# Start and end of a fused attention and feed-forward kernel: another order of loads and values in the first batch, and the last output tile in two column halves

## The chip, the cores and the metric

The kernel runs on one core of a Trainium2 chip. The metric is the device time of one execution in microseconds (us), taken over several runs of which the median is given. A profile of one further execution shows what each engine did: PE is TensorE's matmuls, PEld its weight loads, DVE is VectorE, ACT is ScalarE, POOL is GpSimd, SP is SyncE, which only issues DMAs here.

## The reference

Attention with two kinds of heads, then a feed-forward network without biases. Sizes: 8 batches, 8 heads, 576 positions, head size 64; 4608 tokens, model width 512, inner width 1024. All inputs and the output are float32.

```python
scores = scale * np.matmul(q, k.transpose(0, 1, 3, 2))
rel = pos[:, None] - pos[None, :]
mask_plain = (rel >= 0) & (rel < 32)                       # heads 0 to 3
mask_dil = (rel >= 0) & (rel < 128) & (rel % 4 == 0)       # heads 4 to 7
attn = softmax of the masked scores                        # rows divided by their sum
x = np.matmul(attn, v)          # then to [4608 tokens, 512 channels]
a = x @ w1;  b = x @ w2
out = ((a * b) @ w3) @ w_out
```

## The kernel before

**Attention in steps.** A batch is four steps: `d0`, `d1` (dilated heads, first and second half of the positions) and `p0`, `p1` (plain heads, likewise). The order of positions is permuted so that a dilated head, too, sees a narrow band; each half is then three blocks of 96 queries by 128 keys. A step is: scores on TensorE into PSUM (`score_matmuls`, L275), the exponential on ScalarE into `et`, the values on TensorE (`value_matmul`, L317) with a column of ones beside V that yields the row sum, the division on VectorE (`normalize`: a reciprocal, L324, and a product, L325, into `xo`), and six transposes on TensorE with a copy into the channel-major array `XT` (`to_channels`, L366 and L380). `transpose_qk` brings q and k into head-size-major form on VectorE, four small instructions each, or a single long one (L240) for k of the plain heads.

**Feed-forward.** Tokens are taken 512 at a time, nine tiles. `ffn1` makes a block of 128 features of `a` and `b`, each from four products of 128x512 (L509), multiplied into `gts`; `ffn2` makes 128 tokens of the output from eight products (L560) with `wf_sb`, which is w3 times w_out, computed on the chip once (`fuse_t`, `fuse_m`). ScalarE copies each output tile y to `osb` (L568), and SyncE stores it (L549), in two DMAs where the tile crosses one of the permuted quarters, else in one.

**Order.** The instruction order is written by hand; each engine works through its own list in program order. For batches 1 to 7 the attention work is handed out piece by piece between the products of the feed-forward part (`point`). Batch 0 has nothing to hide behind. It is written out in `first_batch`: there scores and values go in pairs of heads (`scores_of_pair`, `values_of_pair`), and the mask comes in through a product of the identity with a tile of large negative numbers (L291). When XT of the dilated channels is there, four PSUM banks are opened and `begin` computes the half of the first four products that needs only those channels; `ffn1` finishes them later. `begin` of the first feature block stands ahead of `p0.to_channels`, that of the second between it and `p1.to_channels`. Before all that, `warm_up` runs 16 products on constant data while the first loads are under way.

**Queues and buffers.** All loads are issued by GpSimd, in the order in which the main program calls `load_qk`, `load_vd` (V of the dilated heads, four DMAs of pieces of partitions), `load_vp` (V of the plain heads), `load_w12`, and so on; they convert float32 to bfloat16 on the way. Eight semaphores serve these DMAs in turn, so that an issue waits until the DMA eight places ahead has landed. PSUM: one bank `ps_x` for transposes, three banks in rotation handed out by `bank()`, and four that are first the two score buffers `ps_s` (two banks each), then `ps_b` of `begin`, then `ps_a` of the later attention. A bank from `bank()` is free again when the last reader of its former content is done. `et` has three buffers.

Of the kernel before, what the change touches and what calls it, by code (L numbers as in the profile page):

```python
# [10 lines left out]
P = 128  # L11
BF16 = mybir.dt.bfloat16
F32 = mybir.dt.float32
U32 = mybir.dt.uint32
AL = mybir.AluOpType
# [5 lines left out]
D = 64  # L21
# [6 lines left out]
TB = 512  # L28
# [8 lines left out]
def kernel(  # L37
# [11 lines left out]
    nc = tc.nc  # L49
# [6 lines left out]
    KFF = d_ff // P  # L56
    NT = n_tok // TB
# [6 lines left out]
    wk_pool = ctx.enter_context(tc.tile_pool(name="wk", bufs=2))  # L64
# [18 lines left out]
    wf_sb = const.tile([P, KFF, d_model], BF16, name="wf_sb")  # L83
# [16 lines left out]
    ps_x = psum.tile([P, 2 * TB], BF16, name="ps_x")  # L100
    pool = four_banks()
# [3 lines left out]
    def bank():  # L105
        return banks.tile([P, TB], F32, tag="f", name="f")


    qn, kn = {}, {}

    def load_qk(b, us=slice(0, 2)):
        for nm, dst, src in (("qn", qn, q), ("kn", kn, k)):
            if b not in dst:
                dst[b] = qk_pool.tile([P, 2, ROWS * D], BF16, tag=nm, name=nm)
            x = src[b].rearrange("(u h) (j a) d -> (h j) u (a d)", u=2, a=ROWS)
            nc.gpsimd.dma_start(out=dst[b][:, us], in_=x[:, us])  # L116

    def load_vp(b):
        vp = vps[b % NV]
        base = v[b, 0]  # L120

        def rows(p0, n, j0, nj):
            return bass.AP(
                tensor=base.tensor,
                offset=base.offset + (96 * j0 - 32 + p0) * D,
                ap=[[D, n], [96 * D, nj], [1, D]],
            )

        if b < NV:
            nc.gpsimd.dma_start(out=vp[32:P, 0:1, 0:D], in_=rows(32, 96, 0, 1))  # L130
            nc.gpsimd.dma_start(out=vp[:, 1:24, 0:D], in_=rows(0, P, 1, 23))
        else:
            nc.gpsimd.dma_start(out=vp[:, :, 0:D], in_=rows(0, P, 0, 24))

    def load_vd(b):


        x = v[b, 4]
        for m, p0, n, i0, second in ((0, 32, 96, 0, 0), (1, 0, 80, 64, 0), (1, 80, 48, 0, 1), (2, 0, P, 16, 1)):
            nc.gpsimd.dma_start(  # L140
                out=vds[b % 2][p0 : p0 + n, 4 * m : 4 * m + 4, 16 : 16 + 2 * D],
                in_=bass.AP(
                    tensor=x.tensor,
                    offset=x.offset + (4 * i0 + 2 * second) * D,
                    ap=[[4 * D, n], [S * D, 4], [1, 2 * D]],
                ),
            )
# [26 lines left out]

    def warm_up(n):

        ps = bank()
        for _ in range(n):
            nc.tensor.matmul(
                out=ps, lhsT=warm[:, 0:P], rhs=warm, start=True, stop=True  # L180
            )
# [43 lines left out]
    def const_masks():  # L225
        for mask, neg in ((mask_pl, neg_pl), (mask_di, neg_di)):
            nc.vector.tensor_scalar(
                out=mask, in0=neg, scalar1=-1.0, scalar2=None, op0=AL.is_ge
            )


    def transpose_qk(b, u, which):


        src, dst = ((qn, qts), (kn, kts))[which]
        pad = PADK * which
        t = src[b][:, u, :].bitcast(U32).rearrange("p (a i) -> p a i", a=ROWS)
        o = dst[u][b % 2].rearrange("p s c -> p (s c)").bitcast(U32)[:, pad : pad + S]
        if u == 0 and which == 1:
            nc.vector.transpose(out=o.rearrange("p (j a) -> p a j", a=ROWS), in_=t)  # L240
            return
        for a0 in range(4):

            n = 5 - a0 // 2
            at = RES * SLOTS.index(a0)
            step = RES * SLOTS.index((a0 + 2) % 4) + (a0 + 18) // 4 - at
            nc.vector.transpose(  # L247
                out=bass.AP(
                    tensor=o.tensor,
                    offset=o.offset + at,  # L250
                    ap=[o.ap[0], [1, n], [9, 16], [step, 2]],
                ),
                in_=t[:, a0 : a0 + 4 * n - 3 : 4, :],
            )

    class Step:
# [62 lines left out]
            )  # L319

        def normalize(self, ov, xo, n, k):
            rcp = wk_pool.tile([P, n, k], F32, tag=f"rcp{n}", name="rcp")
            ones, x0 = (0, 1) if self.u and self.hf == 0 else (D, 0)
            nc.vector.reciprocal(out=rcp[0:96], in_=ov[0:96, :, :, ones])  # L324
            nc.vector.tensor_tensor(  # L325
                out=xo[0:96].rearrange("p (n k) d -> p n k d", n=n),
                in0=ov[0:96, :, :, x0 : x0 + D],
                in1=rcp[0:96].unsqueeze(3).to_broadcast([96, n, k, D]),
                op=AL.mult,
            )  # L330

        def new_xo(self):
            self.xo = wk_pool.tile([P, 2, 6, D], BF16, tag="xo", bufs=3, name="xo")

        def values_of_pair(self, hp):
            if hp == 0:
                self.new_xo()
            ov = bank()[:, 0 : 6 * (D + 1)].unsqueeze(1)
            ov = ov.rearrange("p n (j e) -> p n j e", e=D + 1)
            for m in range(3):  # L340
                for hl in range(2):
                    self.value_matmul(2 * hp + hl, m, ov[:, 0, 2 * m + hl, :])
            self.normalize(ov, self.xo[:, hp], 1, 6)

        def values(self):


            self.new_xo()
            ov = late["a"][:, :, HALF : HALF + 3 * (D + 1)]
            ov = ov.rearrange("p n (j e) -> p n j e", e=D + 1)  # L350
            for hp in range(2):
                for m in range(3):
                    for hl in range(2):
                        j = 6 * hp + 2 * m + hl
                        self.value_matmul(2 * hp + hl, m, ov[:, j // 3, j % 3, :])
            self.normalize(ov, self.xo.rearrange("p h j d -> p (h j) d"), 4, 3)

        def to_channels(self, ps=ps_x, copy=None):
            xv = ps[:, 0 : 2 * HALF].rearrange("p (h s t) -> p h s t", h=2, s=4)
# [47 lines left out]
    def first_batch():  # L407

        d0, d1, p0, p1 = steps[0:4]
        transpose_qk(0, 1, 0)  # L410
        transpose_qk(0, 1, 1)
        d0.scores_of_pair(0)
        d0.scores_of_pair(1)
        transpose_qk(0, 0, 0)
        transpose_qk(0, 0, 1)
        d1.scores_of_pair(0)
        d1.scores_of_pair(1)
        p0.scores_of_pair(0)
        p0.scores_of_pair(1)
        d0.values_of_pair(0)  # L420
        d0.values_of_pair(1)
        p1.scores_of_pair(0)
        d1.values_of_pair(0)
        p1.scores_of_pair(1)
        d1.values_of_pair(1)
        d0.to_channels()
        p0.values_of_pair(0)
        p0.values_of_pair(1)
        d1.to_channels()
        p1.values_of_pair(0)  # L430
        p1.values_of_pair(1)
        pool = four_banks()
        for f in range(2):
            for i in range(2):
                begin(f, i, pool.tile([P, TB], F32, name=f"ps_b{f}{i}"))
            if f == 0:
                p0.to_channels()
        p1.to_channels(bank().bitcast(BF16), nc.vector.tensor_copy)
        const_masks()
        prefetch(2)  # L440

# [63 lines left out]
    gts = {}  # L505
# [13 lines left out]
    def begin(f, i, ps):  # L519

        begun[f, i] = ps
        ffn1_half(0, f, (w1_sb, w2_sb)[i], (2, 3), begun[f, i])
# [16 lines left out]
                nc.scalar.copy(out=a_sb, in_=ps)  # L539
        nc.vector.tensor_tensor(out=gts[t][:, f], in0=pss[1], in1=a_sb, op=AL.mult)  # L540

    def store(o_sb, r0):
        n = 0
        while n < P:
            b, p = divmod(r0 + n, S)
            slot, i = divmod(p, RES)
            m = min(P - n, RES - i)
            row = b * S + 4 * i + SLOTS[slot]
            nc.sync.dma_start(  # L549
                out=out[row : row + 4 * (m - 1) + 1 : 4, :], in_=o_sb[n : n + m, :]  # L550
            )
            n += m

    def ffn2(t, tb, point):
        point()
        y = bank()
        for f in range(KFF):
            if f == KFF // 2:
                point()
            nc.tensor.matmul(  # L560
                out=y,
                lhsT=gts[t][:, f, tb * P : (tb + 1) * P],
                rhs=wf_sb[:, f, :],
                start=(f == 0),
                stop=(f == KFF - 1),
            )
        o_sb = wk_pool.tile([P, d_model], F32, tag="osb", bufs=6, name="osb")
        nc.scalar.copy(out=o_sb, in_=y)  # L568
        store(o_sb, t * TB + tb * P)

    w3T = {}

# [30 lines left out]
    warm_up(16)  # L603
    load_qk(0, 1)
    const_pool()
    load_qk(0, 0)
    load_vd(0)
    load_vp(0)
    load_w12(0, 256)
    load_w12(256, 512)  # L610
# [24 lines left out]
    def point():  # L635
        state[0] += 1
        want = int(np.ceil(np.interp(state[0], xs, ys)))
        while state[1] < want and (state[1] >= n0 or state[0] >= when[state[1]]):
            for f in phases[state[1]]:
                f()  # L640
            state[1] += 1
# [11 lines left out]
    for tb in range(4):  # L653
        ffn2(0, tb, point)
# [36 lines left out]
```

The softmax here doesn't subtract the row's maximum and nothing guards it: scores larger than these inputs give would overflow.

## Time and profile before

| | us |
|---|---|
| median of 5 runs | 264.15 |
| lowest, highest | 262.93, 266.75 |
| the profiled execution: its own time | 262.93 |
| its span, first to last instruction | 261.2 |
| TensorE busy in the span | 248.5 (95%) |
| start of the dense stream of products | 20.71 |
| end of the last product | 257.04 |

The profiled execution was one of the quicker ones: its own time is 1.2 us under the median, and 1.7 us of it lie outside of the span that the profile shows. All moments below are counted from the span's start. In a row of the timeline the first number is the start, the second the duration, and the bracket tells how long the engine had been idle and what ended that. Ends of matmuls are modelled, so that TensorE's busy time is not time at its peak.

### The profile page before, as it was taken

The numbers are of one execution on the slowest core, as the hardware profiler recorded it, in microseconds if no ns is written. First come the engines' busy times: TensorE is split into PE (matmuls) and PEld (weight loads), VectorE is DVE, ScalarE is ACT, GpSimd is POOL, SyncE is SP. The second block draws the span as 40 slices with busy tenths as digits, with TensorE's granted clock in tenths as the row PEclk, the third lists the DMA queues.
The fourth block names the chain that finished last, engine by engine and source line by source line (L and its number), as shares of the span: only waits on it lengthen the run. The fifth ranks groups of instructions, "written<-read, shape, count | busy, mean of one in ns | idle before, by whom it ended". The sixth has DMA issues, their size and how long they took to land.

```text
span 261.2 us, 5646 instructions
## 1 busy us (share of the span) xinstructions
PE 248.5 (95%) x2332; PEld 126.1 (48%) x2368; DVE 159.2 (61%) x331; ACT 112.4 (43%) x166; POOL 57.8 (22%) x84
## 2 busy tenths in 40 slices
PE   7989989899899999999999999999999999999993
PEld 2454455554455554555555555555554554444441
DVE  6684456967979577857775777578736623412420
ACT  1453335345553455445545554455354324333321
POOL 8962236535261114113311410000000000000000
PEclk9999999999999999999999999999999999999999
DMA  6999999999999959674968591300140021014013
GB/s 104 170 190 209 207 211 200 190 188 228 229 202 165 163 151 109 101 133 130 106 106 154 117 85 43 123 1 4 44 119 0 0 88 75 0 54 110 0 40 121
DMA packets 51817, 30.50 MB, mean 117 GB/s; under 512 B 37968, under 2 KB 42064, under 8 KB 51792
## 3 DMA queue, kind: packets, MB, share of 16 engines
q0 software_dynamic: 46160, 20.70, 63.8%
q1 hardware_dynamic: 5632, 9.44, 11.4%
q8 instruction: 18, 0.29, 0.4%
q14 instruction: 7, 0.06, 0.1%
HBM read 41.39 MB, written 9.44 MB: 195 GB/s over the span
## 4 chain that ended last, share of the span: by engine, by line
PE 84%; DVE 5%; POOL 3%; DMA 3%; issue 2%; ACT 1%; POOLq 0%
PE f L509 45%; PE f L560 23%; PE ps_a L275 4%; PE ps_a L317 4%; PE f L591 3%; PE ps_x L366 3%; DMA w_sb<-in_moe_w_dram 3%; PE ps_b L509 1%; DVE xo L325 1%; POOL vd L140 1%; DVE qt L247 1%; ACT et L305 1%; DVE et L306 1%; DVE kt L240 1%; PE f L577 1%
## 5 line engine op out<-in xcount | busy, mean ns | idle before, releaser
L509 PE MATMUL f<-XT,w_sb 128*128 128x512 bf16 x538 | 128.9, 379 | 1.3 <-issue 0.2
L509 PEld LDWEIGHTS <-w_sb 128*128 128x128 bf16 x576 | 52.8, 98 | 58.7 <-DVE XT L380 0.7
L540 DVE TENSOR_TENSOR gt<-f,asb 128x512 bf16<-128x512 f32 x70 | 48.1, 687 | 39.5 <-PE f L509 35.2
L539 ACT CAST asb<-f 128x512 bf16<-128x512 f32 x70 | 40.9, 585 | 62.6 <-PE f L509 59.8
L560 PE MATMUL f<-wf_sb,gt 128*128 128x512 bf16 x279 | 66.3, 379 | 1.0 <-issue 0.8
L568 ACT COPY osb<-f 128x512 f32<-128x512 f32 x36 | 21.0, 584 | 49.3 <-PE f L560 49.3
L560 PEld LDWEIGHTS <-gt 128*128 128x128 bf16 x288 | 26.3, 98 | 28.2
L305 ACT ACTIVATE et<-ps_a 128x1152 bf16<-128x1152 f32 x28 | 31.7, 1134 | 13.4 <-PE ps_a L275 13.4
L140 POOL DMA_DIRECT2D vd<-in_v_dram x32 | 21.3, 672 | 42.9 <-PE ps_a L317 34.9
L325 DVE TENSOR_TENSOR xo<-ps_a,rcp 96x768 bf16<-96x768 f32 x28 | 26.7, 954 | 1.0
L247 DVE STREAM_TRANSPOSE qt<-qn 128x160 uint32<-128x160 uint32 (+1 forms) x64 | 19.7, 422 | 1.5 <-DMA qn<-in_q_dram 1.5
L317 PEld LDWEIGHTS <-et 128*128 128x128 bf16 x384 | 15.8, 98 | 6.5
L275 PEld LDWEIGHTS <-kt 32*128 32x128 bf16 x768 | 10.9, 93 | 16.1 <-issue 13.1
L306 DVE TENSOR_TENSOR et<-et,mask_pl 128x1152 bf16<-128x1152 bf16 x14 | 10.6, 758 | 11.8 <-ACT et L305 11.8
L306 DVE TENSOR_TENSOR et<-et,mask_di 128x1152 bf16<-128x1152 bf16 x14 | 10.6, 757 | 10.2 <-ACT et L305 10.1
L324 DVE RECIPROCAL rcp<-ps_a 96x12 f32<-96x12 f32 x28 | 6.3, 224 | 16.4 <-PE ps_a L317 16.4
L591 PE MATMUL f<-wo_sb,w3T 128*128 128x512 bf16 x60 | 15.4, 380 | 0.9 <-ACT w3T L583 0.7
L366 PEld LDWEIGHTS <-xo 96*128 96x128 bf16 x192 | 11.5, 97 | 7.5 <-issue 0.5
L275 PE MATMUL ps_a<-qt,kt 32*128 32x96 bf16 x672 | 12.4, 202 | 1.8 <-DVE xo L325 1.5
L366 PE MATMUL ps_x<-ident,xo 96*128 96x96 bf16 x186 | 13.0, 205 | 0.4 <-ACT XT L380 0.4
L380 ACT COPY XT<-ps_x 128x576 bf16<-128x576 bf16 x17 | 10.9, 644 | 2.2 <-PE ps_x L366 2.1
L116 POOL DMA_DIRECT2D qn<-in_q_dram x10 | 6.6, 663 | 21.3 <-DVE qt L247 17.7
(61 smaller groups left out, 140.9 us busy)
## 6 DMA issues: line engine op xcount, KB each, us to landing
qn<-in_q_dram POOLq DMA_DIRECT2D x6, 576.0 KB, 8.0
kn<-in_k_dram POOLq DMA_DIRECT2D x6, 576.0 KB, 9.6
w3n<-in_moe_w_dram POOLq DMA_DIRECT2D x4, 512.0 KB, 15.6
out_dram<-osb SPq DMA_DIRECT2D x8, 256.0 KB, 2.3
vp<-in_v_dram POOLq DMA_DIRECT2D x5, 384.0 KB, 6.4
out_dram<-osb SPq DMA_DIRECT2D x8, 224.0 KB, 2.7
out_dram<-osb SPq DMA_DIRECT2D x8, 192.0 KB, 2.9
out_dram<-osb SPq DMA_DIRECT2D x8, 160.0 KB, 2.4
```

The costliest lines, as they stand in the source:

```text
L140: nc.gpsimd.dma_start(out=vds[b % 2][p0 : p0 + n, 4 * m : 4 * m + 4, 16 : 16 + 2 * D], in_=bass.AP(tensor=x.tensor, offset=x.offset + (4 * ...
L275: nc.tensor.matmul(out=bank_of(h)[:, c0 : c0 + 96], lhsT=kt[prt, 96 * m : 96 * m + P, c], rhs=rhs, start=(start and c == 0), stop=(c == 1 ...
L305: nc.scalar.activation(out=ev, in_=ps_a[:, :, 0:HALF], func=ACT.Exp, scale=scale)
L306: nc.vector.tensor_tensor(out=ev, in0=ev, in1=mk.unsqueeze(1).to_broadcast([P, 4, HALF]), op=AL.mult)
L317: nc.tensor.matmul(out=out, lhsT=self.et[:, c0 : c0 + P], rhs=rhs, start=True, stop=True)
L325: nc.vector.tensor_tensor(out=xo[0:96].rearrange("p (n k) d -> p n k d", n=n), in0=ov[0:96, :, :, x0 : x0 + D], in1=rcp[0:96].unsqueeze(3) ...
L366: nc.tensor.transpose(out=xo, in_=self.xo[0:96, hp, 2 * m : 2 * m + 2, :], identity=ident[0:96, 0:96],)
L509: nc.tensor.matmul(out=ps, lhsT=w_sb[:, c, f * P : (f + 1) * P], rhs=XT[:, c, t * TB : (t + 1) * TB], start=(c == 2), stop=(c == 1),)
L539: nc.scalar.copy(out=a_sb, in_=ps)
L540: nc.vector.tensor_tensor(out=gts[t][:, f], in0=pss[1], in1=a_sb, op=AL.mult)
L560: nc.tensor.matmul(out=y, lhsT=gts[t][:, f, tb * P : (tb + 1) * P], rhs=wf_sb[:, f, :], start=(f == 0), stop=(f == KFF - 1),)
L591: nc.tensor.matmul(out=wf_ps[ft], lhsT=w3T[ft][:, g, :], rhs=wo_sb[:, g, :], start=(g == 0), stop=(g == KFF - 1),)
```

## The change

It has four parts, in the first 21 us and at the very end.

1. The main program issues the loads of batch 0's upper half (the plain heads) as q, then V of the dilated heads, then k; before, it was q, k, V.
2. `first_batch` has another order. The values of both dilated steps come ahead of the transpose of the plain k and of all plain scores; four more warm-up products follow, and the warm-up writes to `ps_x` instead of a rotating bank. `d0.to_channels` copies on VectorE instead of ScalarE and stands between the plain scores. `begin` of the second feature block is split: its first part stands between `p0.to_channels` and `p1.to_channels`, its second behind both.
3. `values_of_pairs` takes both pairs of heads of a step: values and reciprocal of the first pair, values and reciprocal of the second, then the two products. The reciprocals get four buffers.
4. `ffn2` makes the last 128 tokens in two halves of 256 columns, each with its own eight products, its own copy and its own store.

```diff
@@ load_qk
-    def load_qk(b, us=slice(0, 2)):
-        for nm, dst, src in (("qn", qn, q), ("kn", kn, k)):
+    def load_qk(b, us=slice(0, 2), which=(0, 1)):
+        for nm, dst, src in [(("qn", qn, q), ("kn", kn, k))[i] for i in which]:
@@ warm_up
-        ps = bank()
+        ps = ps_x.bitcast(F32)
@@ normalize
-            rcp = wk_pool.tile([P, n, k], F32, tag=f"rcp{n}", name="rcp")
+            rcp = wk_pool.tile([P, n, k], F32, tag=f"rcp{n}", bufs=4, name="rcp")
             ones, x0 = (0, 1) if self.u and self.hf == 0 else (D, 0)
             nc.vector.reciprocal(out=rcp[0:96], in_=ov[0:96, :, :, ones])
-            nc.vector.tensor_tensor(
...
+            def products():
+                nc.vector.tensor_tensor(
...
+            return products
@@ values_of_pair
-        def values_of_pair(self, hp):
...
+        def values_of_pairs(self):
+            self.new_xo()
+            products = []
+            for hp in range(2):
+                ov = bank()[:, 0 : 6 * (D + 1)].unsqueeze(1)
+                ov = ov.rearrange("p n (j e) -> p n j e", e=D + 1)
+                for m in range(3):
+                    for hl in range(2):
+                        self.value_matmul(2 * hp + hl, m, ov[:, 0, 2 * m + hl, :])
+                products.append(self.normalize(ov, self.xo[:, hp], 1, 6))
+            for f in products:
+                f()
@@ first_batch
         d0.scores_of_pair(0)
         d0.scores_of_pair(1)
         transpose_qk(0, 0, 0)
-        transpose_qk(0, 0, 1)
         d1.scores_of_pair(0)
         d1.scores_of_pair(1)
+        d0.values_of_pairs()
+        transpose_qk(0, 0, 1)
+        d1.values_of_pairs()
+        warm_up(4)
         p0.scores_of_pair(0)
         p0.scores_of_pair(1)
-        d0.values_of_pair(0)
-        d0.values_of_pair(1)
+        d0.to_channels(ps_x, nc.vector.tensor_copy)
         p1.scores_of_pair(0)
-        d1.values_of_pair(0)
+        p0.values_of_pairs()
         p1.scores_of_pair(1)
-        d1.values_of_pair(1)
-        d0.to_channels()
-        p0.values_of_pair(0)
-        p0.values_of_pair(1)
         d1.to_channels()
-        p1.values_of_pair(0)
-        p1.values_of_pair(1)
+        p1.values_of_pairs()
         pool = four_banks()
-        for f in range(2):
-            for i in range(2):
-                begin(f, i, pool.tile([P, TB], F32, name=f"ps_b{f}{i}"))
-            if f == 0:
-                p0.to_channels()
+        ps_b = [pool.tile([P, TB], F32, name=f"ps_b{i}") for i in range(4)]
+        begin(0, 0, ps_b[0])
+        begin(0, 1, ps_b[1])
+        p0.to_channels()
+        begin(1, 0, ps_b[2])
         p1.to_channels(bank().bitcast(BF16), nc.vector.tensor_copy)
+        begin(1, 1, ps_b[3])
@@ store, ffn2
-    def store(o_sb, r0):
+    def store(o_sb, r0, cols):
...
+        last = t == NT - 1 and tb == 3
         o_sb = wk_pool.tile([P, d_model], F32, tag="osb", bufs=6, name="osb")
-        nc.scalar.copy(out=o_sb, in_=y)
-        store(o_sb, t * TB + tb * P)
+        for c0, n in ((0, 256), (256, 256)) if last else ((0, 512),):
+            point()
+            y = bank()[:, 0:n]
+            for f in range(KFF):
...
+                    rhs=wf_sb[:, f, c0 : c0 + n],
...
+            nc.scalar.copy(out=o_sb[:, c0 : c0 + n], in_=y)
+            store(o_sb, t * TB + tb * P, slice(c0, c0 + n))
@@ main program
     load_qk(0, 1)
     const_pool()
-    load_qk(0, 0)
+    load_qk(0, 0, (0,))
     load_vd(0)
+    load_qk(0, 0, (1,))
     load_vp(0)
```

More of the change, by code (lines that the diff above doesn't have):

```diff
@@ L321, in normalize @@
         def normalize(self, ov, xo, n, k):
-            rcp = wk_pool.tile([P, n, k], F32, tag=f"rcp{n}", name="rcp")
+            rcp = wk_pool.tile([P, n, k], F32, tag=f"rcp{n}", bufs=4, name="rcp")
             ones, x0 = (0, 1) if self.u and self.hf == 0 else (D, 0)
             nc.vector.reciprocal(out=rcp[0:96], in_=ov[0:96, :, :, ones])
-            nc.vector.tensor_tensor(
[L326 to L330, printed above, removed]
+            def products():
+                nc.vector.tensor_tensor(
+                    out=xo[0:96].rearrange("p (n k) d -> p n k d", n=n),
+                    in0=ov[0:96, :, :, x0 : x0 + D],
+                    in1=rcp[0:96].unsqueeze(3).to_broadcast([96, n, k, D]),
+                    op=AL.mult,
+                )
+            return products
         def new_xo(self):
             self.xo = wk_pool.tile([P, 2, 6, D], BF16, tag="xo", bufs=3, name="xo")
-        def values_of_pair(self, hp):
[L336 to L343, printed above, removed]
+        def values_of_pairs(self):
[10 more added lines that the diff above has]
+                f()
         def values(self):
@@ L355, in values @@
                         self.value_matmul(2 * hp + hl, m, ov[:, j // 3, j % 3, :])
-            self.normalize(ov, self.xo.rearrange("p h j d -> p (h j) d"), 4, 3)
+            self.normalize(ov, self.xo.rearrange("p h j d -> p (h j) d"), 4, 3)()
         def to_channels(self, ps=ps_x, copy=None):
@@ L549, in store @@
             nc.sync.dma_start(
-                out=out[row : row + 4 * (m - 1) + 1 : 4, :], in_=o_sb[n : n + m, :]
+                out=out[row : row + 4 * (m - 1) + 1 : 4, cols], in_=o_sb[n : n + m, cols]
             )
@@ L554, in ffn2 @@
     def ffn2(t, tb, point):
[L555 to L566, printed above, removed]
-        o_sb = wk_pool.tile([P, d_model], F32, tag="osb", bufs=6, name="osb")
-        nc.scalar.copy(out=o_sb, in_=y)
-        store(o_sb, t * TB + tb * P)
+        last = t == NT - 1 and tb == 3
+        o_sb = wk_pool.tile([P, d_model], F32, tag="osb", bufs=6, name="osb")
+        for c0, n in ((0, 256), (256, 256)) if last else ((0, 512),):
+            point()
+            y = bank()[:, 0:n]
+            for f in range(KFF):
+                if f == KFF // 2 and not last:
+                    point()
+                nc.tensor.matmul(
+                    out=y,
+                    lhsT=gts[t][:, f, tb * P : (tb + 1) * P],
+                    rhs=wf_sb[:, f, c0 : c0 + n],
+                    start=(f == 0),
+                    stop=(f == KFF - 1),
+                )
+            nc.scalar.copy(out=o_sb[:, c0 : c0 + n], in_=y)
+            store(o_sb, t * TB + tb * P, slice(c0, c0 + n))
     w3T = {}
```

## The prediction

> **What bounds the kernel now.** I read the page first, then the busy time by stage, the chain of waits over the first 24 us, the timeline of that stretch with the landings of its loads, and last the end. On the page the columns are busy time, share of the span, count; its fourth part shares the span out along the chain that ended last:
>
> ```profile
> PE 248.5 (95%) x2332; PEld 126.1 (48%) x2368; DVE 159.2 (61%) x331; ACT 112.4 (43%) x166; POOL 57.8 (22%) x84
> PE 84%; DVE 5%; POOL 3%; DMA 3%; issue 2%; ACT 1%; POOLq 0%
> ```
>
> TensorE is the bound. Cut where the change cuts (begin, length, then busy time and count per engine):
>
> ```profile
> 0.00:20.71 20.71, 17.18 (x207) 9.11 (x209) 13.79 (x57) 8.29 (x12) 16.52 (x30) 1.00 1.27 158
> 20.71:257.04 236.33, 231.34 (x2125) 116.95 (x2160) 145.36 (x275) 103.54 (x153) 41.24 (x54) 1.00 0.72 113
> 257.04:261.20 4.16, 0.00 (x0) 0.00 (x0) 0.00 (x0) 0.58 (x1) 0.00 (x0) 0.86 0.31 108
> ```
>
> In the middle, 236.33 us, TensorE is 98% busy, and the change alters no instruction in it but the very last eight products. So only two dates count: when the dense stream of 128x512 products begins (20.71), and how long the end takes after the last product (4.16). The chain of waits for the start:
>
> ```profile
> 4.59 0.54 POOL kn L116
> 5.13 2.65 POOL vd L140 x4
> ...
> 10.83 7.29 DMA w_sb<-in_moe_w_dram
> 18.12 0.05 issue
> 18.17 0.60 PE ps_b L509 x2
> 18.78 0.26 PE ps_x L366 x6
> 19.03 0.86 PE ps_b L509 x4
> 19.90 0.27 PE f L366 x6
> 20.17 0.02 issue
> 20.19 0.47 DVE XT L380
> 20.66 0.05 issue
> 20.71 1.90 PE ps_b L509 x8
> ```
>
> The second half of the first weights lands at 18.12; from there TensorE runs without a gap to 20.16 and then waits 0.55 us for the last copy into XT. Behind it two more rows of the timeline (start, duration, idle before in brackets):
>
> ```profile
> 10.56 1.26 DVE L240 STREAM_TRANSPOSE kt<-kn 128x576 uint32<-128x576 uint32 x1 [0.97 <-DMA kn<-in_k_dram]
> 13.36 0.19 DVE L324 RECIPROCAL rcp<-f 96x6 f32<-96x6 f32 x1 [1.53 <-PE f L317]
> ```
>
> VectorE transposes k of the plain heads when it lands, 10.56, and then idles 1.53 us: the first values need vd and stand on TensorE behind the plain scores. From 13.36 it runs eight reciprocal-and-product pairs at 0.69 us up to 18.97. The landings, from issue (7.0 for the last vd, 4.58 for k):
>
> ```profile
> kn<-in_k_dram POOLq DMA_DIRECT2D x1, 288.0 KB, 6.0
> vd<-in_v_dram POOLq DMA_DIRECT2D x1, 128.0 KB, 5.5
> ```
>
> So k is there at 10.56, vd at 12.5. The end:
>
> ```profile
> 257.07 0.58 ACT L568 COPY osb<-f 128x512 f32<-128x512 f32 x1 [1.14 <-PE f L560]
> 257.68 0.35 SPq L549 DMA_DIRECT2D out_dram<-osb  x1
> out_dram<-osb SPq DMA_DIRECT2D x1, 256.0 KB, 2.6
> ```
>
> copy 0.58, store 2.6 from issue to landing (to 260.24), 0.92 of closing work.
>
> **What the Trainium skill says.** "DMA: Bandwidth & Descriptors", Queues, rings and completion order: each DMA engine consumes descriptors in ring order. The trace agrees: q, k, q, k, vd land in the order of issue, so swapping issues swaps landings. The same page, Anatomy of one DMA, gives a DMA about 2 us of fixed cost, mostly the receipt of the last write. The trace agrees: near the end a 32 KB store lands 2.1 us after issue, one of 256 KB 2.6. "TensorE: Matmul & The Clock Gate", Part 1, says that an idle TensorE falls to half clock and wins full clock only after about 3.4 us of work. The trace agrees on the two speeds: the first warm-up products start 0.427 us apart, the products from 18.17 on 0.216. No re-throttling is seen in this start.
>
> **The change, part by part.**
>
> *Loads.* q, vd (four DMAs), k in place of q, k, vd: same bytes, same queue. k's 288 KB at the 200 GB/s of this stretch are 1.44 us, so vd lands at about 12.5 - 1.45 = 11.05 and k at about 12.4 to 12.6, where vd was. vp and the weights keep their places: vp at 15.3, the second weight at 18.1. The wait of 0.26 us that GpSimd had for kn before that weight's issue goes; its landing is set by the transfers ahead, so I count nothing.
>
> *Values of the dilated heads first.* TensorE leaves the d1 scores at about 10.85; d0's values start with vd at 11.0 instead of 12.96 (12 products, 0.55), d1's behind them.
>
> *Products behind both reciprocals.* A pair costs 0.18 + 0.035 + 0.55 less 0.08 of overlap with the next, 0.69. Two reciprocals and then two products hide one dependent gap and one overlap more: about 1.2 us for 1.38. Four such groups: 0.7 us of VectorE. Against it, the first product now waits for the second group of values: 0.2 for d0 (0.55 - 0.36), and for p1 until its second exponential is done. d1's second bank waits for d0's first product; TensorE has only the warm-up queued behind it.
>
> *k's transpose* now stands on VectorE behind d0's products: first reciprocal 11.4, end of group about 12.65, k landed by then; transpose 12.65 to 13.9. Four warm-up products (4 x 0.216 = 0.86, about 12.5 to 13.4) end before it and cost nothing; they fill TensorE's idle time and would cost up to 0.5 us only if k were there at 12.0. The plain scores start at 13.95 where they started at 11.88: 2.07 later. Here lies the price of the change.
>
> *From there, with the durations of before.* Each pair of scores holds TensorE 0.71, its exponential starts 0.47 after its first score product (11.88 to 12.35) and takes 0.65. p0: exponentials at 14.4 and 15.15. d0's six transposes at 15.0 (0.25, copy on VectorE from 15.5), p1's first scores 15.3, p0's values 16.0 (vp is there at 15.3), p1's second scores 16.4, exponential 17.2 to 17.87; d1's transposes 17.1, their copy on ScalarE behind that exponential, 17.8 to 18.4. VectorE: d1 group to 15.1, copy to 15.95, p0 group 16.4 to 17.75, p1's second reciprocal 18.3, products to 19.55. The first `begin` starts at 18.45, now held by XT and not by the weight (18.1). TensorE then has 4 products (0.86), 6 transposes (0.25), 2 products (0.43), 6 transposes (0.25, drain 0.17): 20.4; copy 0.46 and two handovers of 0.05: dense stream at 20.98. The last two `begin` products lie under that copy, where before 0.55 us were idle. Sum at the start: 20.98 - 20.71 = +0.27, with -0.45 to +0.8 as the ends (below). It cannot win more than about 0.46: w2 for feature block 4 lands at about 26.3, and its first use is at 26.76 today.
>
> *Last y in halves.* 8 products of 512 columns become 16 of 256: same streaming time, 8 weight loads more (98 ns each, overlapped; the transposes start 0.042 apart with a load each, under the 0.108 that 256 columns take). The first half's copy and store lie beside the second half's products. On the path stays a copy of 256 columns: exponentials of 576 and 1152 columns take 0.650 and 1.134, so 0.84 ns a column, 0.215 us saved. The store halves to 128 KB in as many, shorter packets: between nothing (if packets count) and 0.5 (if bytes do: 32 to 160 KB land in 2.0 to 2.1). I take 0.4. SyncE is free (the first half's issue, 0.35, is over by 257.2). Sum at the end: -0.6, from -0.2 to -0.75.
>
> **Sum.** 262.93 us was the profiled execution's own time (span 261.2, 1.7 around it). +0.27 - 0.6 = -0.33: 262.6. The median of the five runs is 1.22 above that execution, so 263.8.
>
> **Rivals.**
> *The start shortens as well.* If vd lands by 10.85 and the groups pack tighter, XT is ready by 17.9, the weight at 18.12 is the bound again and the dense stream begins at 20.26: -0.45. With the end -1.05: 263.1. For it: 1.53 us of idle VectorE and 0.55 of idle TensorE go. Against it: plain scores two microseconds later.
> *k comes too late (slower).* Place: k's transpose, the only thing between VectorE and all plain scores. It decides from a landing of about 13.0: until 12.65 d0's products hide it, and 0.33 more eats the net gain. For it: V arrives in short lines, and the 380 KB of vp took 2.8 us behind vd, slower than k or q. At 13.6 the net is +0.6: 264.4; a p1 chain later than mine adds to the same sum, to about 264.8.
> *TensorE turns cold.* Between 11 and 14 it has some 1.6 us of work in 3. A half-clock window of 3.4 us during the begin products loses 1.7: 265.5. For it: the change adds warm-up products, just there. Against: no window stays idle.
> *The end does not shorten*: receipt and packet count rule, -0.2 only: 264.2.
>
> **How the numbers follow.** My forecast 0.50, its own range 263.2 to 264.5; start shorter 0.17; late k 0.15; cold 0.08; end unchanged 0.10. The range 262.4 to 265.5 takes in all five, and a median of five that wanders by some 0.7 (the runs spread from 262.93 to 266.75). About 1% is what a measurement of this kernel can tell from no change: under 261.5 or over 266.8. No case reaches the first, since start and end together can give 1.2; the cold case with a high median reaches the second. Faster 0.07, same 0.82, slower 0.11.
>
> **What would show it.** In the new profile: vd landed near 11, kt's transpose at about 12.65 behind d0's products with no wait on DMA over 0.2; the first `begin` at 18.4 behind ScalarE's XT copy; dense stream at 20.98; the last copy near 0.37 and its store landing about 2.1 after issue, so that the stretch behind the last product falls from 4.16 to about 3.55. A wait of kt on kn of half a microsecond or more, begin products 0.43 apart, or a last store still at 2.6 would prove me wrong, each in its term.

## The result, and the profile after

| | before | changed |
|---|---|---|
| median, us | 264.88 (45 runs) | 263.16 (24 runs) |
| lowest, highest, us | 262.93, 266.75 | 262.64, 264.50 |
| profiled execution: its own time, its span, us | 262.93, 261.16 | 263.11, 261.34 |

The ratio to before is 0.9936, 95% interval 0.9919 to 0.9954: faster, by 1.7 us in the medians, and inside the 1% that I called no change. The ratios in this document leave out runs that lie 1.5% above the quickest of their kernel; the medians are over all runs. Since runs came from more than one chip, each kernel is compared with the runs of before made beside it.

The table holds a riddle. Between the two profiled executions nothing is gained: 262.93 against 263.11. The median falls because the changed kernel's runs lie together, and those of before do not. The stages after, with the same columns as for before (begin and end, length, then busy time and count of each engine, granted clock, DMA):

```profile
0.00:21.29 21.29, 17.53 (x210) 9.29 (x213) 13.79 (x58) 7.65 (x11) 16.61 (x31) 1.00 1.26 159
21.29:257.50 236.21, 231.29 (x2133) 117.79 (x2168) 145.46 (x275) 103.91 (x154) 41.14 (x54) 1.00 0.72 113
257.50:261.34 3.84, 0.00 (x1) 0.00 (x0) 0.00 (x0) 0.37 (x1) 0.00 (x0) 1.00 0.35 117
```

The start is 0.58 us longer than before's 20.71, the middle the same to 0.12, the end 0.28 shorter (4.12 from the modelled end of the last product before). The chain of waits of the start:

```profile
4.57 2.63 POOL vd L140 x4
7.20 5.68 DMA kn<-in_k_dram
12.88 0.02 issue
12.91 1.26 DVE kt L240
...
18.08 0.64 ACT XT L388
18.73 0.04 issue
18.77 0.38 PE ps_b L515
...
20.78 0.47 DVE XT L388
21.25 0.05 issue
21.29 1.90 PE ps_b L515 x8
```

The chain now runs through k: V of the dilated heads, k, its transpose, all of the plain steps. The first `begin` product starts at 18.77, right behind ScalarE's copy into XT; the second half of the weights had landed at 18.19, so no `begin` product waits for it any more. The wait for k, from the timeline:

```profile
12.91 1.26 DVE L240 STREAM_TRANSPOSE kt<-kn 128x576 uint32<-128x576 uint32 x1 [0.43 <-DMA kn<-in_k_dram]
```

And the end: the timeline, and from the DMA issues the last store's size and its time from issue to landing:

```profile
257.54 0.37 ACT L578 COPY osb<-f 128x256 f32<-128x256 f32 x1 [0.50 <-PE f L571]
257.94 0.35 SPq L555 DMA_DIRECT2D out_dram<-osb  x1
```

```profile
out_dram<-osb SPq DMA_DIRECT2D x1, 128.0 KB, 2.1
```

Copy 0.58 to 0.37, store 2.6 to 2.1: both as the prediction had them, 0.7 us together. Yet only 0.28 arrives.

### The profile page after: what moved, and what is told of

Its sections match the earlier page's. It is cut to its first block, busy times and chain, and to the rows that moved or that the text cites. A ratio compares the mean times of both kernels' runs of the same rounds, so it can differ in the third digit from the quotient of the medians.

```text
span 261.3 us, 5673 instructions
## 1 busy us (share of the span) xinstructions
PE 248.8 (95%) x2343; PEld 127.1 (49%) x2380; DVE 159.3 (61%) x332; ACT 111.9 (43%) x166; POOL 57.8 (22%) x84
## 3 DMA queue, kind: packets, MB, share of 16 engines
q0 software_dynamic: 46160, 20.70, 63.9%
## 4 chain that ended last, share of the span: by engine, by line
PE 85%; DVE 5%; DMA 2%; POOL 2%; issue 2%; ACT 2%; POOLq 0%; ACTq 0%
PE f L515 45%; PE f L571 23%; PE ps_a L275 4%; PE ps_a L317 4%; PE f L601 3%; PE ps_x L374 3%; DMA kn<-in_k_dram 2%; PE ps_b L515 1%; DVE xo L328 1%; DVE kt L240 1%; POOL vd L140 1%; DVE qt L247 1%; ACT et L305 1%; DVE et L306 1%; PE ps_s L275 1%
## 5 line engine op out<-in xcount | busy, mean ns | idle before, releaser
L571 PE MATMUL f<-wf_sb,gt 128*128 128x512 bf16 (+1 forms) x287 | 66.3, 373 | 1.0 <-issue 0.8
L578 ACT COPY osb<-f 128x512 f32<-128x512 f32 (+1 forms) x37 | 21.2, 573 | 49.0 <-PE f L571 48.7
L571 PEld LDWEIGHTS <-gt 128*128 128x128 bf16 x296 | 27.1, 98 | 27.6
L305 ACT ACTIVATE et<-ps_a 128x1152 bf16<-128x1152 f32 x28 | 31.7, 1134 | 13.4 <-PE ps_a L275 13.3
L275 PEld LDWEIGHTS <-kt 32*128 32x128 bf16 x768 | 10.9, 92 | 16.7 <-issue 13.1
L275 PE MATMUL ps_a<-qt,kt 32*128 32x96 bf16 x672 | 12.4, 202 | 1.8 <-DVE xo L328 1.5
L388 ACT COPY XT<-ps_x 128x576 bf16<-128x576 bf16 x16 | 10.3, 644 | 1.5 <-PE ps_x L374 1.4
## 6 DMA issues: line engine op xcount, KB each, us to landing
w3n<-in_moe_w_dram POOLq DMA_DIRECT2D x4, 512.0 KB, 16.3
```

The costliest lines, as they stand in the source:

```text
L275: nc.tensor.matmul(out=bank_of(h)[:, c0 : c0 + 96], lhsT=kt[prt, 96 * m : 96 * m + P, c], rhs=rhs, start=(start and c == 0), stop=(c == 1 ...
L305: nc.scalar.activation(out=ev, in_=ps_a[:, :, 0:HALF], func=ACT.Exp, scale=scale)
L571: nc.tensor.matmul(out=y, lhsT=gts[t][:, f, tb * P : (tb + 1) * P], rhs=wf_sb[:, f, c0 : c0 + n], start=(f == 0), stop=(f == KFF - 1),)
```

## The experiments

There were two questions. Why do the runs of before scatter and those of the changed kernel not? And where does the end lose 0.4 us? My theory for the first was the clock. Each run lists the granted TensorE clock as a mean over the execution. Of the changed kernel's 25 runs, the profiled one included, 15 had 0.999 or 1.000, and its four slowest had 0.990 to 0.994. Below, "low clock" is a mean under 0.9955. The mark follows from a sum: the drops found below last 3.41 us at half clock, and half of 3.41 is 0.0065 of a span of 261 us, so one drop takes the mean to about 0.9935. A drop behind the last product costs no time and takes about 0.002 (before's profile: 0.998).

### The kernel before, again; and the changed kernel without its four products

First the kernel before, unchanged:

> The kernel before, unchanged, to see what its own runs differ by. The profile of before was of its quickest execution (262.93 us), while its median is 264.88. Clock theory: the runs above 264 us show a mean granted TensorE clock under 0.995, because TensorE falls to half clock somewhere in the first 21 us, and a profile of such a run shows a second stretch at half clock there: 1.5 to 3 us long, with the dense stream beginning 1 to 3 us after 20.7. Rival, loads: the clock is 1.00 in all runs and the slower ones differ by late landings of q, k, V or the weights. Ratio to before 1.000 either way.

Then the changed kernel with one edit:

```diff
         d1.values_of_pairs()
-        warm_up(4)
         p0.scores_of_pair(0)
```

> The changed kernel without its four extra warm-up products. Clock theory: it is these products that keep TensorE at full clock between 11 and 14 us; without them the runs scatter as those of before do, mean clock under 0.995 in many, median 264 to 265, ratio 0.997 to 1.003. Rival, order: the gain comes from the order of loads and values; the four products lie in idle time and taking them away changes nothing, ratio 0.993 to 0.995, clock 1.00.

Measured, e1: ratio 0.9989 (0.9962 to 1.0015), median 264.77, 8 of 14 runs at low clock. e2: ratio 1.003 (1.0001 to 1.0059), median 265.89, 13 of 14 at low clock. Without the four idle products the new order of loads and values is not a gain, and by its interval rather a small loss.

Both profiles caught a drop. Stretches of 3.41 us, counted from the moment when the clock rose, in e1; the numbers behind the five engines are clock, DMA share, GB/s:

```profile
10.02:13.43 3.41, 2.91 (x62) 1.77 (x62) 1.66 (x3) 2.51 (x4) 3.41 (x5) 1.00 2.13 161
13.43:16.84 3.41, 1.91 (x49) 1.42 (x46) 2.31 (x7) 1.83 (x3) 1.56 (x3) 1.00 1.55 180
16.84:20.26 3.42, 3.35 (x33) 2.10 (x33) 2.71 (x8) 0.64 (x1) 2.10 (x3) 0.50 1.42 198
```

TensorE is busy 1.91 of 3.41 us, and for the next 3.41 us it gets half the clock, just when the `begin` products come. The same stretches in the changed kernel and, second, in e2, whose clocks rose within 0.03 us of each other:

```profile
9.51:12.92 3.41, 2.75 (x54) 1.85 (x55) 1.51 (x6) 1.58 (x3) 3.41 (x6) 1.00 1.69 168
12.92:16.33 3.41, 2.72 (x52) 1.59 (x51) 2.76 (x6) 1.30 (x2) 2.75 (x4) 1.00 1.74 182
16.33:19.75 3.42, 2.94 (x52) 1.99 (x52) 2.54 (x8) 1.83 (x3) 1.53 (x3) 1.00 1.44 197
```

```profile
9.53:12.94 3.41, 2.52 (x52) 1.59 (x52) 1.60 (x6) 1.55 (x3) 3.41 (x6) 1.00 1.70 169
12.94:16.36 3.42, 2.39 (x57) 1.69 (x58) 2.49 (x6) 1.46 (x3) 2.85 (x4) 1.00 1.70 180
16.36:19.77 3.41, 3.41 (x41) 2.15 (x38) 2.13 (x8) 1.67 (x3) 1.44 (x2) 0.50 1.42 198
```

Same order, same phase of the clock, and with the four products 0.2 to 0.3 us more of work in each of the first two stretches, and no drop. That is one execution of each; the counts weigh more. On the chip of e2, 13 of 14 runs had low clock without the products, and in e3 (below), with them and the end of before, 1 of 10.

The mean clock also tells the size of a drop. Of 186 runs of before made beside e1 to e12, 91 had low clock: 18 lay at 0.990 to 0.994, 29 at 0.984 to 0.987 and 44 at 0.980 or 0.981. At 0.0065 for each drop that would be, as an estimate, one, two and three of them. The last group had a median of about 266.2 on each of the three chips, the other two 264.8 to 265.0. Every profile here with a drop in its start (e1, e2, e5, e9) shows a single one, so where the slowest runs lose their time no trace shows.

### The start alone, the end alone

```diff
-        last = t == NT - 1 and tb == 3
+        last = False
```

> The changed start with the end of before (last y in one piece). The end is worth about 0.3 us between the two profiles (4.12 to 3.84 us behind the last product), so: clock theory, where the start steadies the clock, median 263.4 to 263.6, ratio 0.994 to 0.996, scatter as small as that of the changed kernel. Rival, the end is what is gained: median 264.6, ratio near 1.000.

The end alone is before with the changed `store` and `ffn2`:

```diff
-    def store(o_sb, r0):
+    def store(o_sb, r0, cols):
...
+        for c0, n in ((0, 256), (256, 256)) if last else ((0, 512),):
```

> The kernel before with the last y in two column halves and nothing else. Clock theory: 0.3 us less than before in every run and the same scatter, ratio 0.998 to 1.000. Rival, the end is what is gained: ratio 0.993 to 0.996. In the profile the last store lands about 2.06 us after issue for 2.56, but some 0.4 us are lost behind it, as in the changed kernel, where SyncE checks seven more semaphores after the last landing.

e3: ratio 0.9938 (0.991 to 0.9965), median 263.26, 1 of 10 runs at low clock. e4: 0.9989 (0.9961 to 1.0018), median 264.63, 7 of 14 at low clock. So the start makes the difference; the end's 0.28 us is there in the profile of e4 (last stretch 3.83, in e3 4.12), but below what the runs resolve.

In the profile of e3 k landed in time, at 12.53; three steps of its chain of waits:

```profile
12.56 1.26 DVE kt L240
18.42 1.02 PE ps_b L515 x4
20.94 1.90 PE ps_b L515 x8
```

The prediction had 12.65, 18.45 and 20.98.

### Four products in the old order, early, late, and both

The warm-up writes to `ps_x` in all three.

```diff
         d1.scores_of_pair(1)
+        warm_up(4)            # e5, e10
         p0.scores_of_pair(0)
...
         d1.values_of_pair(1)
+        warm_up(4)            # e6, e10
         d0.to_channels()
```

> The kernel before with four warm-up products (into ps_x) behind the scores of d1, where TensorE waits for the transpose of k, about 10.8 to 11.7 us. In the run of e1 that was profiled the clock halved at 16.84 for one window of 3.41 us, so the window that decided is 13.43 to 16.84. Theory A, the clock is decided by the work in the last window before the drop: products at 11 lie in most phases a window too early, the scatter stays mostly as it was, ratio 0.997 to 1.002. Theory B, any extra work in this start steadies the clock: ratio 0.993 to 0.995, clocks 1.00.

> The kernel before with four warm-up products behind the values of d1, ahead of d0's transposes, about 15.2 to 16.0 us. They cost 0.2 to 0.5 us of the path in a run at full clock. Theory A (the last window decides): most drops near 16 to 17 go, ratio 0.994 to 0.998. Theory B: ratio 0.993 to 0.997 too, so that this run with e5 tells the two apart. Rival to both, that the order of loads and values and not the warm-up steadies the clock: ratio 1.000 to 1.003, as the products are only added work.

> The kernel before with four warm-up products behind the scores of d1 and four more behind the values of d1 (about 10.5 to 11.5 and 15.2 to 16). In two of the five profiles of the old order V of the plain heads landed at 16.6 and 16.7 instead of 14.8 to 15.3, TensorE waited for it and the clock halved in that window. Clock theory: with both groups no window is thin, clocks 1.00 in nearly all runs, ratio 0.994 to 0.997. Late V as a cause of its own: clocks 1.00, but a second group of runs 1 to 1.5 us above the first stays, ratio 0.997 to 1.001.

| | ratio (interval) | median | low clock |
|---|---|---|---|
| e5, early | 0.9984 (0.9961 to 1.0008) | 263.59, before 264.50 | 5 of 22 |
| e6, late | 1.0004 (0.9975 to 1.0033) | 264.01, before 264.50 | 5 of 22 |
| e10, both | 0.9981 (0.9961 to 1.0002) | 263.61, before 264.10 | 0 of 22 |

Each group alone cuts the share of low-clock runs from about half to less than a quarter; in e10 none is left, where before beside it had 34 of 72. By these shares theory A, that only work in the last window counts, isn't borne out: early products help as often as late ones. The sizes differ, though: the five low-clock runs of e5 had 0.990 to 0.994, those of e6 0.984 to 0.987. The ratios alone decide nothing: all three intervals include 1, e5's ratio lies where theory A had it, and e6's where the rival of both theories had it.

None of the three becomes as quick as the changed kernel, but they lack its end. Beside e5, e8 (below: the changed start, and an end 0.35 us shorter than before's) has a median of 263.20, 0.39 less. Beside e10, e12 (an end 0.72 us shorter) has 262.98, 0.63 less. So the medians don't show that the changed start is quicker than four or eight products in the old order.

In e10 every run had full clock and the median still lay 0.45 us above before's own full-clock runs on that chip (263.16). The profile of e10 shows what else can hold up the old order, V of the plain heads. Its issue to landing among the DMAs, and in the timeline who waits, down to the first product of the dense stream:

```profile
vp<-in_v_dram POOLq DMA_DIRECT2D x1, 368.0 KB, 8.3
```

```profile
16.64 0.49 PE L317 MATMUL f<-vp,et 128*128 128x65 bf16 x11 [0.26 <-DMA vp<-in_v_dram]
19.30 0.11 PEld L511 LDWEIGHTS <-w_sb 128*128 128x128 bf16 x2 [0.99 <-DMA w_sb<-in_moe_w_dram]
21.84 1.47 PE L511 MATMUL ps_b<-XT,w_sb 128*128 128x512 bf16 x6 [0.55 <-DVE XT L380]
```

It landed at 16.6 (issue 8.26), the second weight behind it at 19.3 instead of 18.1, and the dense stream began at 21.84. In the profiles of the old order with an early V, before, e4 and e6, it began at 20.71, 20.93 and 20.70. e6 has the late products too, so it isn't they that cost this microsecond. In e1 the wait was longer:

```profile
16.75 0.71 PE L317 MATMUL f<-vp,et 128*128 128x65 bf16 x11 [1.50 <-DMA vp<-in_v_dram]
```

In six profiles of the old order (before, e1, e4, e5, e6, e10) this load landed at 15.3, 16.7, 14.8, 16.6, 14.8 and 16.6: two groups. The old order asks for it at 14.9 to 15.6 (e10: 16.2), and in three of the six, e1, e5 and e10, TensorE waited. In e1 and e5 that wait fell into the very stretch ahead of the drop; here is e5:

```profile
14.80:18.22 3.42, 2.06 (x51) 1.75 (x46) 2.42 (x8) 1.84 (x4) 1.17 (x2) 1.00 1.43 192
18.22:21.63 3.41, 3.18 (x13) 1.21 (x13) 1.57 (x5) 0.64 (x1) 2.00 (x3) 0.50 1.32 204
```

So in e1 and e5 a late V and the drop came together. The dense stream of e1 began at 22.39, only 0.55 later than that of e10, which had late V and full clock: set side by side, these two profiles give late V the larger part of e1's delay. The seven profiles with the new order and the new loads have V at 15.0 to 16.3, and ask for it at 15.9 to 16.8: no one waits.

### Seven products instead of four

```diff
-        warm_up(4)
+        warm_up(7)
```

> The changed kernel with seven instead of four extra warm-up products. TensorE idles from 13.5 to 14.2 us in the changed kernel, waiting for k's transpose; three more products (0.65 us) fill it. Clock theory: the remaining runs with a clock of 0.990 to 0.994 (263.9 to 264.5 us) go, median 263.0 to 263.2, ratio 0.992 to 0.994, highest under 263.7. Rival: four are enough and the rest comes from elsewhere, or the three delay the plain scores: median 263.2 to 263.5, highest unchanged.

Ratio 0.9956 (0.9933 to 0.9979), median 263.30, 1 of 22 runs at low clock; highest 264.91. The ratio misses the 0.992 to 0.994 of the clock theory. There are fewer drops than in the changed kernel (4 of 25) and in e8, which has four products and ran on the same chip (6 of 22), but the median is no better, and the counts are too small to call the share different.

### The old loads under the new order

```diff
-    load_qk(0, 0, (0,))
+    load_qk(0, 0)
     load_vd(0)
-    load_qk(0, 0, (1,))
```

> The changed kernel with the old order of loads (q, k, V of the dilated heads), all else as changed. V lands near 12.5 instead of 10.9, and VectorE takes k's transpose behind d0's products, so the whole start moves by about 1.5 us: dense stream at 22.5 to 23. Theory, the loads are needed for the new order: ratio 0.999 to 1.004. Rival, the warm-up alone makes the gain and the loads are indifferent: ratio 0.993 to 0.996.

Ratio 1.0048 (1.0016 to 1.0081), median 265.48, all 19 runs at low clock. V lands at 12.8 and all of TensorE waits for it; the stretch up to the drop:

```profile
10.49:13.91 3.42, 1.25 (x28) 0.86 (x22) 0.79 (x4) 0.83 (x2) 2.96 (x5) 1.00 2.17 158
13.91:17.32 3.41, 3.12 (x24) 1.64 (x26) 2.71 (x7) 0.00 (x1) 2.75 (x5) 0.50 1.48 189
```

The warm-up products come too late here, at 14.7, and run at half clock themselves; the dense stream begins at 23.94. The expectation was 22.5 to 23; the drop was not in it. The new order needs the new loads.

### Products right behind their reciprocals

```diff
-                products.append(self.normalize(ov, self.xo[:, hp], 1, 6))
-            for f in products:
-                f()
+                self.normalize(ov, self.xo[:, hp], 1, 6)()
```

> The changed kernel with each product right behind its own reciprocal, as before. The prediction put two reciprocals and then two products at 1.2 us for 1.38 and the first product later. If pairing is worth its 0.2 us a group on the path, the dense stream begins 0.2 to 0.6 us later (21.4 to 21.9) and the ratio is 0.994 to 0.996. Rival: VectorE is not what the start waits for (late k, scores, exponentials), the dense stream stays within 0.15 us of 21.29, ratio 0.993 to 0.995.

Ratio 0.998 (0.9951 to 1.0009), median 263.52, 7 of 22 at low clock; the ratio lies in neither of the expected ranges, and the stream's 21.74 in the one that I had given to pairing. But in its profile k landed late, and VectorE waited twice as long for it:

```profile
13.36 1.26 DVE L240 STREAM_TRANSPOSE kt<-kn 128x576 uint32<-128x576 uint32 x1 [0.84 <-DMA kn<-in_k_dram]
21.74 2.27 PEld L512 LDWEIGHTS <-w_sb 128*128 128x128 bf16 x12 [0.61 <-DVE XT L385]
```

From the transpose of k to the dense stream 21.74 - 13.36 = 8.38 us; in the changed kernel 21.29 - 12.91 = 8.38. So in these profiles pairing the products is worth nothing on the path, and the later stream comes from the later landing. VectorE has time to spare: in the changed kernel it idles 0.45 us or more before three of the four groups, and 0.53 us behind the other. The runs fit: at full clock e11 has a median of 263.44 and e12, on the same chip, 262.88, of which the shorter end accounts for 0.44.

### The end: which semaphore the last store has

SyncE's stores use eight semaphores in turn, and before the program ends it checks all eight in order. 64 stores give the last one the last semaphore. The changed kernel issues 65, the last gets the first semaphore, and seven checks, 0.06 us apart in its trace from 260.01 to 260.44, stand behind its landing at 259.99. Two ways to have 64 again:

```diff
-            store(o_sb, t * TB + tb * P, slice(c0, c0 + n))
+            store(o_sb, t * TB + tb * P, slice(c0, c0 + n),
+                  nc.gpsimd if last and c0 == 0 else nc.sync)
```

> The changed kernel with the store of the first column half of the last y issued by GpSimd instead of SyncE, so that SyncE issues 64 stores as before and the last one again has the last of its eight semaphores. Semaphore theory: the 0.43 us of seven checks behind the last landing (260.04 to 260.47) go in front of it; from the end of the last product to the end of the span 3.4 us for 3.84, and 0.3 to 0.5 us off the median, 262.7 to 262.9, ratio 0.991 to 0.993. Rival: the closing checks are not on the path or GpSimd's store lands later than SyncE's: the stretch stays at 3.8 or grows.

```diff
-            nc.sync.dma_start(
+            queue = nc.gpsimd if r0 == (NT - 1) * TB and n else nc.sync
+            queue.dma_start(
```

> The changed kernel with one earlier store, the 48 rows of the first 128 tokens of the last tile, issued by GpSimd instead of SyncE, some 5 us before the end: SyncE then issues 64 stores and the last has the last of its eight semaphores, without a second store beside it as in e8. Semaphore theory: last landing 2.06 us after issue as in the changed kernel, and 0.95 to 1.0 us from there to the end of the span for 1.35; behind the last product 3.4 to 3.5 us for 3.84; median 262.7 to 262.9, ratio 0.991 to 0.993. Rival: the closing checks are hidden: 3.8 us as in the changed kernel.

e8: ratio 0.9941 (0.9914 to 0.9968), median 263.20, 6 of 22 at low clock. The checks went in front, but the last landing came later, 2.3 us after issue for 2.1; the end is 3.77 for 3.84. What is different is that the store of the other half comes from GpSimd. That a second store is under way can't be the reason: in the changed kernel one is too, from SyncE, issued at 257.28 and landed at 259.53. e12, where the store given to GpSimd lies 5 us earlier, in its timeline, its DMA issues and its last stretch:

```profile
258.00 0.37 ACT L579 COPY osb<-f 128x256 f32<-128x256 f32 x1 [0.50 <-PE f L572]
258.40 0.35 SPq L556 DMA_DIRECT2D out_dram<-osb  x1
```

```profile
out_dram<-osb SPq DMA_DIRECT2D x1, 128.0 KB, 2.0
```

```profile
257.96:261.36 3.40, 0.01 (x1) 0.00 (x0) 0.00 (x0) 0.37 (x1) 0.00 (x0) 0.91 0.40 133
```

The last stretch is 3.40 us, 0.44 less than in the changed kernel, as the theory said. The ratio is not in the 0.991 to 0.993 that went with it: 0.9968 (0.9944 to 0.9993), median 262.98 against 264.10 of before beside it, 6 of 22 at low clock. Its median is the lowest of all kernels; that it beats the changed kernel was not measured side by side, only the stretch shows it.

## Why the prediction was right, and where not

**Time and sign.** 263.16 lies inside 262.4 to 265.5, faster and under 1%, as forecast; it lies just under the 263.2 to 264.5 that the forecast had as its own range. The sum that led there, -0.33, is not what the median did, -1.7. That the time fell inside is owed to the width of the range, and so in part to luck: what gained stood in no term of the sum.

**The step that was mis-sized** is the last line of the sum: "The median of the five runs is 1.22 above that execution, so 263.8". It carried before's scatter over to the changed kernel as if it were noise of the measurement. It is a property of the start: the scatter stays with the old start (e4) and goes with the new one (e3). On the three chips before's low-clock runs had medians of 265.4 to 265.8, its full-clock runs 263.2 to 264.2. The changed kernel had 4 low-clock runs of 25; with e3, e8 and e12, which have the same start, 17 of 79.

How much of the gain is the clock? An estimate from the means: low-clock runs raise before's mean above that of its full-clock runs by 0.7, 1.0 and 1.0 us on the chips of e1 to e4, e5 to e8 and e9 to e12, and the mean of the kernel with the changed start beside it (e3, e8, e12) by 0.1, 0.45 and 0.4. That leaves 0.6 us on each chip. It is not surely the clock's alone, since in the old order late V came with the drop in e1 and e5. What is left differs by chip. On the first, e3 at full clock has a median of 263.24 against 264.22 of before. On the others there is 263.10 (e8) against 263.56 and 262.88 (e12) against 263.16, where the shorter ends alone would make 0.35 and 0.72. I put the first down to late V, which the new order no longer waits for. That is not shown: the only profile of the old start at full clock from that chip, e4, had its V early.

**The cold rival** had the right mechanism on the wrong kernel. I asked whether the changed kernel's idle stretch would turn TensorE cold, and did not ask whether before already did; "No re-throttling is seen in this start" was true of the one execution shown, the quickest of its kernel. That an idle TensorE falls to half clock, as the prediction has it, does not cover what is seen here: it fell behind stretches in which it was busy for 37% (e9) to 70% (e2) of the time. The price of 1.7 us was too high for the new start: from k's transpose to the dense stream the profile of e2, with one drop, has 21.91 - 12.65 = 9.26 us for 8.38, and low-clock runs at 0.990 to 0.994 have medians 0.8 to 0.9 us above the full-clock ones (changed kernel, e8, e12). The four products that I booked as "cost nothing" are the part that pays: without them the ratio is 1.003.

**The start**, +0.27 forecast, came out at +0.58 between the profiles, and at +0.23 in e3 (20.94). V of the dilated heads landed at 10.9 (11.05 forecast), good. The mechanism held, and k's landing was a little mis-sized: 12.88 in the changed kernel, not 12.4 to 12.6 (e3: 12.53). It decides from 12.5 on, where d0's products end, as the slower rival said: the transpose started at 12.91 for 12.65. The rest of the chain held to 0.05: transpose to dense stream 8.38 us, forecast 20.98 - 12.65 = 8.33. In e11 and e12 k landed at 13.3 and 13.4, and the stream moved with it, to 21.74 and 21.77. Pairing's 0.2 us a group exists in VectorE's time (1.28 us for the group at 16.67, 1.45 for two pairs at 15.44 before), but not on the path.

**The end**, -0.6 forecast, -0.28 measured. Copy 0.21 saved, as said; store 0.5, I took 0.4. What the sum lacked is the wait behind the landing: the extra store turns the order of the closing checks, 0.44 us (e12). It could have been read beforehand from the number of stores.

**What stays open.** What decides whether the clock falls. Busy time of the stretch before does not decide alone: in e2 a stretch with 2.39 of 3.42 us busy led to half clock, in e12 one with less did not:

```profile
11.55:14.97 3.42, 1.68 (x23) 0.96 (x24) 2.28 (x6) 0.00 (x0) 3.34 (x5) 1.00 2.03 160
14.97:18.38 3.41, 3.41 (x79) 2.32 (x73) 2.44 (x7) 2.31 (x4) 1.66 (x3) 1.00 1.47 196
```

e12's stretch held the 512-column warm-up products on all rows, e2's small products, many of them on 32 rows; that weight of work per busy time matters is likely, but not shown. Nor is it settled why V of the plain heads lands in two groups in the old order, 1.3 to 1.9 us apart, or where the runs with a mean clock of 0.980 to 0.987 lose theirs. And no run joins the old order and its idle products to the new end, which would tell what the new order itself is worth.

## What to carry to other kernels

Look at the mean granted clock of every run and at the scatter before a profile is taken for the kernel: the profiled execution can be the quick one, and a change that gains nothing there can gain 1.7 us in the median. Where a start consists of small products with waits between them, a few idle products put into a wait that exists anyway are cheap insurance: eight of them took the low-clock runs of the old order from 34 of 72 to none of 22. Whether reordering adds to that has to be measured with everything else equal. When a store or another DMA is split, count which semaphore the last one gets, and what is checked behind it.

## What the runs showed of the hardware

- After it has risen, the TensorE clock can fall back to half inside a running kernel, for 3.41 us (16.84 to 20.26 in e1, 16.36 to 19.77 in e2, 18.22 to 21.63 in e5, 13.91 to 17.32 in e9), although TensorE was busy for 56%, 70%, 60% and 37% of the stretch before. In these traces it rose at 6.60, 6.12, 4.56 and 7.08; each fall comes 2, 3 or 4 times 3.41 us later. The moment of the first rise differs from run to run (4.1 to 7.5 us in these profiles).
- Closing checks of semaphores cost 0.06 us each when they stand behind the last landing (seven in the changed kernel, 0.44 us; e12 without them).
- With one 128 KB store from SyncE and one from GpSimd in flight, the last landed 2.3 us after issue (e8); with both from SyncE, 2.0 to 2.1 (changed kernel, e12).
